# Token halves of K and V exchanged for half the units, so that 32-wide matmuls use eight array quadrants

## The chip, the cores and the metric

The kernel runs on one core of one Trainium2 chip. The metric is device time in microseconds (us), lower is better. Before the change three runs took 635.24, 636.76 and 638.88 us; their median is 636.76.

## The reference

Two stages follow each other. The first is a delta rule over 768 tokens for 4 batches and 8 heads of dimension 48, in fp32:

```python
k_n = k / (np.linalg.norm(k, axis=-1, keepdims=True) + 1e-06)
for t in range(S):
    y[:, :, t] = q[:, :, t] @ state
    v_old = state . k_n[:, :, t]
    state = state + beta * outer(k_n[:, :, t], v[:, :, t] - v_old)
```

The second is a gated MLP on the 3072 rows of y (width 384, inner width 1536): `out = (sigmoid(x @ w_gate) * (x @ w_val)) @ w_out`.

## The kernel before, in words

The 768 tokens are cut into N = 12 groups of 64. In a group there are 32 units (batch and head), named by e (0, 1), x (0, 1) and j (0 to 7); `tokens_at(e, x)` says on which half of the 128 partitions a unit's 64 tokens lie. Within a group the recurrence is written as matrix products, solved in two halves of 32 tokens:

- `gram` (line 282): K times K transposed into `pg` (line 291, 32 matmuls of 64x64). ACT copies its diagonal blocks to G (six copies, line 303) and its lower left blocks to L (four copies, line 308).
- `masked` (line 311): K times Q transposed into `pp` (line 319); DVE writes it back under a causal mask (line 324, four operations).
- `norms` and `solve` (DVE, lines 235 and 329): lengths of K, then the inverse of a triangular 32x32 matrix per unit and half, by some 62 small operations; the last one (line 352) transposes the result into `mt`.
- `rest` (line 434): K times the state into `pk` (line 446); `less` (line 454) subtracts it from V, which gives R.
- `updates` (line 459) in three steps. Step 0, the first U product: `mt` times R for the first 32 tokens into `pu` (line 477), copied to `su` by four ACT copies (line 483). Step 1, the L product: L times that U is added onto `pk` for the other 32 tokens (line 469), then `less` again. Step 2, the second U product.
- `rows` (line 485): Y. One kind of unit (x = 1) adds two products (line 503); the other (x = 0) has query and masked matrix stacked on 128 rows and is one matmul of 128 rows by 64 columns each (line 506, 16 matmuls).
- `advance` (line 514): the new state through `pd` (line 524).
- `turn` or `flip`: Y transposed into the MLP's input.

A matmul of 32 rows by 32 columns uses one of the array's sixteen 32x32 quadrants: its row block is given by where the operands lie, its column block by where the result goes. In steps 0 to 2 the 32 matmuls of a step go round four quadrants, since the four kinds (e, x) have four different row blocks and each always writes to one column block.

The MLP is what fills PE between these steps. A group has 24 slots: in an even slot `gate_val` (line 586) makes one tile of gate and value (`gv`, 18 matmuls), in an odd slot `outp` (line 617) adds one tile to the output (`po`, 6 matmuls). The sigmoid (ACT, line 591), the product (DVE, line 592), the split in two parts (ACT line 597, DVE line 602) follow it. The MLP of a group runs one group behind the recurrence. The order is written by hand: `plan[s]` holds what is issued in slot s right behind the matmuls, `late[s]` what comes last in it. From group 4 on, counted in slots of a period: `gram` of the next group and `rest` in slot 6, U in 9, L and the next group's `masked` in 11, the second U in 13, Y and the state in 15. Each engine works its own list off in order.

[...]

Of the kernel before, what the change touches and what calls it, by code (L numbers as in the profile page):

```python
# [12 lines left out]
F32 = mybir.dt.float32  # L13
# [8 lines left out]
PSUM = bass.MemoryType.PSUM  # L22

B, H, S, D = 4, 8, 768, 48
C = 64
GT = B * C
N = S // C
# [9 lines left out]
def tokens_at(e, x):  # L37
    return 64 * e if x else 64 - 64 * e


def head_of(e, x, j):

    return j // 2, (j % 2) * 4 + x * 2 + e
# [12 lines left out]
def deltanet_gated_mlp(ctx: ExitStack, tc: tile.TileContext, kd, qd, kv, beta, words, out):  # L56
# [4 lines left out]
    wt = ctx.enter_context(tc.tile_pool(name="wt", bufs=1))  # L61
    wk = ctx.enter_context(tc.tile_pool(name="wk", bufs=1))
    ps_seq = ctx.enter_context(tc.tile_pool(name="ps_seq", bufs=2, space=PSUM))
    ps_aux = ctx.enter_context(tc.tile_pool(name="ps_aux", bufs=2, space=PSUM))
    ps_gv = ctx.enter_context(tc.tile_pool(name="ps_gv", bufs=2, space=PSUM))
    ps_out = ctx.enter_context(tc.tile_pool(name="ps_out", bufs=2, space=PSUM))

# [214 lines left out]
    def gram(g):  # L282

        kq, st = kqp[g % 2], state[g]
        st["G"] = G = wk.tile([128, 32, CP], F32, name=f"G_{g}", tag="G", bufs=1)
        st["L"] = L = wk.tile([128, CP, 32], F32, name=f"L_{g}", tag="L", bufs=2)
        pg = [ps_aux.tile([128, J, C], F32, name=f"pg_{g}_{e}", tag="aux") for e in range(2)]
        for j in range(J):
            for e, x in KINDS:
                r, t = 64 * e, tokens_at(e, x)  # L290
                nc.tensor.matmul(out=pg[e][t:t + 64, j], lhsT=kq[r:r + D, x, j], rhs=kq[r:r + D, x, j], start=True, stop=True)  # L291
        return blocks_of(pg, G, L, g == 0)

    def blocks_of(pg, G, L, halves):
        for e in range(2):
            js = slice(e * J, (e + 1) * J)

            for lo, hi, o in ((0, 128, 0), (32, 64, 32), (96, 128, 32)):
                block = pg[e][lo:hi, :, o:o + 32].rearrange("q p t -> q t p")
                if halves and e:  # L300
                    nc.vector.tensor_copy(out=G[lo:hi, :, js], in_=block)
                else:
                    nc.scalar.copy(G[lo:hi, :, js], block)  # L303
                yield
        for e in range(2):
            for t in (0, 64):
                lo, o = t + 32 * e, 32 - 32 * e
                nc.scalar.copy(L[lo:lo + 32, e * J:(e + 1) * J], pg[e][lo:lo + 32, :, o:o + 32])
                yield

    def masked(g):

        kq = kqp[g % 2]
        pool, tag = (ps_aux, "aux") if g else (ps_out, "po")
        pp = [pool.tile([128, J, C], F32, name=f"pp_{g}_{e}", tag=tag) for e in range(2)]
        for j in range(J):
            for e, x in KINDS:
                r, t = 64 * e, tokens_at(e, x)
                nc.tensor.matmul(out=pp[e][t:t + 64, j], lhsT=kq[r:r + D, x, j], rhs=kq[r:r + D, 3 if x else 2 + 2 * e, j], start=True, stop=True)  # L319

        def masks():
            for e, x in sorted(KINDS):
                t, sec = tokens_at(e, x), 5 if x else 2 + 2 * e
                nc.vector.tensor_tensor(out=kq[t:t + 64, sec], in0=pp[e][t:t + 64],  # L324
                                        in1=pmask[t:t + 64, e].unsqueeze(1).to_broadcast([64, J, C]), op=ALU.mult)
                yield
        return masks()
# [45 lines left out]
    def solve_halves(g):  # L373
# [29 lines left out]
        pool, tag = (ps_aux, "aux") if g else (ps_gv, "gv")  # L403
        pz, pm = (pool.tile([128, CP, 32], F32, name=f"{n}_{g}", tag=tag) for n in ("pz", "pm"))

        def blocks(out, lhsT, rhs):
            for c in range(CP):
# [51 lines left out]
    def updates(g, step):  # L459

        st = state[g]
        R, L = st["R"], st["L"]

        at = {(e, x): [tokens_at(e, x) + 32 * (k ^ e) for k in range(2)] for e, x in KINDS}
        if step == 1:
            for j in range(J):
                for e, x in KINDS:
                    one, two = at[e, x]
                    nc.tensor.matmul(out=st["pk"][e][two:two + 32, j], lhsT=L[one:one + 32, e * J + j], rhs=su[one:one + 32, 3 if x else e, j],  # L469
                                     start=False, stop=True, skip_group_check=True)  # L470
            less(g)
            return
        pu = [ps_aux.tile([128, J, D], F32, name=f"pu_{g}_{step}_{x}", tag="aux") for x in range(1 if g else 2)]
        for j in range(J):
            for e, x in KINDS:
                r = at[e, x][step // 2]
                nc.tensor.matmul(out=pu[0 if g else x][r:r + 32, j], lhsT=mt[r:r + 32, e * J + j], rhs=R[e][r:r + 32, j], start=True, stop=True)  # L477
        for e, x in KINDS:
            r = at[e, x][step // 2]
            if g == 0 and x:  # L480
                nc.vector.tensor_copy(out=su[r:r + 32, 3 if x else e], in_=pu[1][r:r + 32])
            else:
                nc.scalar.copy(su[r:r + 32, 3 if x else e], pu[0][r:r + 32])  # L483

    def rows(g):

        st = state[g]
        kq = kqp[g % 2]

        py = [ps_aux.tile([128, 2, H // 2, D], F32, name=f"yy_{g}_{e}", tag="aux") for e in range(2)]  # L490

        def out_of(e, x, j):
            b, h = head_of(e, x, j)
            lo = 64 * (b % 2)
            return py[e][lo:lo + 64, b // 2, h // 2]
        order = [4 * hf + 2 * c + i for hf in range(2) for i in range(2) for c in range(2)]
        for pair in zip(order[::2], order[1::2]):
            for part in range(2) if g else (1,):
                for j in pair:
                    for e in range(2):  # L500
                        r = 64 * e
                        lhsT, rhs = ((kq[r:r + D, 3, j], su[r:r + D, 2, j]), (kq[r:r + 64, 5, j], su[r:r + 64, 3, j]))[part]
                        nc.tensor.matmul(out=out_of(e, 1, j), lhsT=lhsT, rhs=rhs, start=part == 0 or g == 0, stop=part == 1)  # L503
        for e in range(2):
            for j in order:
                nc.tensor.matmul(out=out_of(e, 0, j), lhsT=kq[:, 2 + 2 * e, j], rhs=su[:, e, j], start=True, stop=True)  # L506
# [26 lines left out]
    def flip(g, c):  # L533

        st = state[g]
        if c == 0:
            xx = wk.tile([128, 2, KC, GT], F32R if g else F32, name=f"xx_{g}", tag=f"xx{(g + 1) % 2}", bufs=1)
            st["xh"], st["xl"] = (xx[:, i] for i in range(2))
        xh, xl, ys = st["xh"], st["xl"], st["ys"][:, c].rearrange("p h e d -> p (h e d)")
        pt = ps_aux.tile([128, KC, 128], F32, name=f"pt_{g}_{c}", tag="aux")  # L540
# [209 lines left out]
    def mask_later(g, s):  # L750
        def fn():
            masks = masked(g)
            take(masks, 2)
            plan[s + 1].insert(0, steps(masks, 2))
        late[s].append(fn)
        for i in range(2):
            busy[s + i] += 1.4

    def gram_later(g, s):
        def fn():  # L760
            copies = gram(g)
# [120 lines left out]
```

## Time and profile before

| | |
|---|---|
| median of three runs | 636.76 us |
| the profiled execution's own time | 635.61 us |
| its span, first to last instruction | 633.9 us |
| PE, busy share of the span | 97% |
| mean granted PE clock | 0.998 |
| DMA, mean rate | 65 GB/s |

Times in the views are counted from the span's start. PE is TensorE's matmuls, PEld its weight loads, DVE VectorE, ACT ScalarE. A line of a group of instructions gives source line, engine, operation, output and inputs, shape, count, then busy time in us and the mean of one in ns, then the idle time ahead of them and what ended it. A row of the timeline begins with start and length in us; in the table of stretches the first numbers are the length and PE's busy time. An fp32 matmul appears as two records, so a step of 32 matmuls counts 64.

### The profile page before, as it was taken

The page shows a single profiled execution, that of the slowest core. Times are in us where ns is not written, and L with a number is a line of the kernel's source. Part 1 is how long each engine was busy: PE and PEld are TensorE (multiplying, and loading weights), DVE is VectorE, ACT ScalarE, POOL GpSimd, SP SyncE. Part 2 cuts the span into 40 slices and gives each one's busy share as a digit, 9 for nine tenths or more (in the row PEclk, how much of TensorE's full clock was granted, in tenths as well). Part 3 has the DMA queues.
Part 4 walks back from the last instruction along what each step waited for, and adds up shares of the span by engine and source line. Part 5 has one row for each costly group of instructions (what it writes and reads, how often), then busy time and mean ns, then how long its engine had stood idle before and what let it go on. Part 6 is the DMA issues. An engine that isn't in the chain of part 4 may idle for free.

```text
span 633.9 us, 24057 instructions
## 1 busy us (share of the span) xinstructions
PE 614.6 (97%) x10494; PEld 571.2 (90%) x10502; DVE 476.8 (75%) x1443; ACT 344.0 (54%) x933; POOL 39.6 (6%) x102
## 2 busy tenths in 40 slices
PE   6689999999999999999999999999999999999996
PEld 4367778989999999999999999999999999999996
DVE  5888897589977977977977977977987977953221
ACT  4879865567356356356355355355455455445222
POOL 6000000000002002002002002002002002001000
PEclk9999999999999999999999999999999999999999
DMA  9495831202203203103102102102112100100101
GB/s 271 177 296 181 277 91 54 53 2 87 52 3 86 52 4 86 42 12 86 45 11 86 34 21 87 27 28 86 26 29 86 26 4 3 26 3 2 26 1 25
DMA packets 17769, 41.06 MB, mean 65 GB/s; under 512 B 4224, under 2 KB 7296, under 8 KB 17664
## 3 DMA queue, kind: packets, MB, share of 16 engines
q1 hardware_dynamic: 17664, 39.53, 21.5%
q8 instruction: 82, 1.34, 0.9%
q14 instruction: 23, 0.19, 0.1%
HBM read 34.80 MB, written 4.72 MB: 62 GB/s over the span
## 4 chain that ended last, share of the span: by engine, by line
PE 91%; DVE 5%; ACT 1%; issue 1%; DMA 1%; ACTq 0%; SPq 0%; DVEq 0%
PE gv L586 45%; PE po L617 22%; PE gv L583 5%; PE pu L477 3%; PE po L611 3%; PE yy L503 2%; PE yy L506 2%; PE pk L446 2%; PE pg L291 2%; PE pp L319 2%; PE pd L524 2%; PE pk L469 1%; PE pm L409 1%; ACT su L483 1%; DVE kqp L324 1%
## 5 line engine op out<-in xcount | busy, mean ns | idle before, releaser
L586 PE MATMUL gv<-xx,w 128*128 128x256 f32 x2376 | 311.2, 285 | 0.0
L586 PEld LDWEIGHTS gv<-xx,w 128*128 128x128 f32 x2376 | 298.8, 191 | 3.1
L617 PE MATMUL po<-w,h 128*128 128x384 f32 x792 | 161.9, 340 | 0.0
L617 PEld LDWEIGHTS po<-w,h 128*128 128x128 f32 x792 | 133.8, 188 | 0.8
L597 ACT CAST h<-sg 128x256 fp32r<-128x256 f32 x132 | 53.5, 405 | 120.1 <-DVE sg L592 119.0
L591 ACT ACTIVATE sg<-gv 128x256 f32<-128x256 f32 x144 | 54.7, 380 | 107.8 <-PE gv L586 98.5
L592 DVE TENSOR_TENSOR sg<-sg,gv 128x256 f32<-128x256 f32 x144 | 60.1, 417 | 67.3 <-ACT sg L591 66.5
L350 DVE TENSOR_TENSOR X<-X,tmp 128x126 f32<-128x126 f32 (+22 forms) x279 | 71.1, 255 | 8.3
L347 DVE TENSOR_TENSOR tmp<-X,gp 128x126 f32<-128x126 f32 (+22 forms) x279 | 71.0, 254 | 8.3
L602 DVE TENSOR_TENSOR h<-sg,h 128x256 fp32r<-128x256 f32 x132 | 56.4, 428 | 13.2 <-ACT h L597 13.2
L562 POOL COPY x<-yt 32x192 f32<-32x192 f32 x72 | 28.3, 393 | 450.3 <-DVE yt L557 447.6
L279 ACT ACTIVATE kv<-kv,mq 128x48 f32<-128x48 f32 x192 | 47.9, 324 | 0.0
L483 ACT COPY su<-pu 32x384 f32<-32x384 f32 x92 | 43.3, 470 | 5.9 <-PE pu L477 4.1
L583 PE MATMUL gv<-xx,u 128*128 128x256 f32 x144 | 33.8, 385 | 0.7 <-issue 0.4
L324 DVE TENSOR_TENSOR kqp<-pp,pmask 64x512 f32<-64x512 f32 x48 | 32.3, 687 | 2.1 <-PE pp L319 1.1
L303 ACT COPY G<-pg 32x256 f32<-32x256 f32 (+1 forms) x69 | 25.3, 367 | 14.0 <-PE pg L291 12.7
L583 PEld LDWEIGHTS gv<-xx,u 128*128 128x128 f32 x144 | 26.6, 190 | 5.8 <-issue 0.8
L557 DVE STREAM_TRANSPOSE yt<-ys 128x768 f32<-128x768 f32 x9 | 8.8, 979 | 25.4 <-ACT ys L512 25.4
L457 DVE TENSOR_TENSOR R<-kv,pk 128x384 f32<-128x384 f32 x44 | 22.3, 549 | 6.6 <-PE pk L469 6.5
L562 ACT COPY x<-yt 32x192 f32<-32x192 f32 x72 | 25.2, 349 | 1.2
L212 ACT CAST w<-u 128x384 fp32r<-128x384 f32 x36 | 18.0, 508 | 8.1 <-DVE w L219 8.0
L531 DVE TENSOR_TENSOR su<-su,pd 48x384 f32<-48x384 f32 x40 | 21.7, 543 | 0.8 <-PE pd L524 0.4
(109 smaller groups left out, 556.2 us busy)
## 6 DMA issues: line engine op xcount, KB each, us to landing
raw<-in_words_dram SPq DMA_DIRECT2D x36, 384.0 KB, 5.5
kv<-in_kv_dram SPq DMA_DIRECT2D x24, 384.0 KB, 4.5
kqp<-in_qd_dram SPq DMA_DIRECT2D x24, 256.0 KB, 4.1
kqp<-in_kd_dram SPq DMA_DIRECT2D x24, 192.0 KB, 3.5
out_dram<-ot SPq DMA_DIRECT2D x48, 96.0 KB, 2.2
beta<-in_beta_dram SPq DMA_DIRECT2D x12, 16.0 KB, 4.0
```

Of the source, the lines that this page charges most:

```text
L279: nc.scalar.activation(V[:, c], V[:, c], AF.Copy, scale=mq[:, c, 0:1])
L347: nc.vector.tensor_tensor(out=tmp, in0=X[:, k:16, j:j + 1].to_broadcast([128, n, j]), in1=gp[:, j:j + 1, 0:j].to_broadcast([128, n, j]), o ...
L350: nc.vector.tensor_tensor(out=X[:, k:16, 0:j], in0=X[:, k:16, 0:j], in1=tmp, op=ALU.add)
L483: nc.scalar.copy(su[r:r + 32, 3 if x else e], pu[0][r:r + 32])
L562: copy(x[32 * q:32 * q + 32, :, :, a].rearrange("q k c s -> q c k s"), yt[32 * a:32 * a + 32, :, q::4])
L583: nc.tensor.matmul(out=pg[:, o], lhsT=parts[w, f][:, k * 128:(k + 1) * 128], rhs=x[0][:, k], start=k == 0, stop=k == KC - 1)
L586: nc.tensor.matmul(out=pg[:, o], lhsT=parts[w, f][:, a, k * 128:(k + 1) * 128], rhs=x[b][:, k], start=(k == 0 and q == 0), stop=(k == KC - ...
L591: nc.scalar.activation(h, st["gv", f][:, 0], AF.Sigmoid)
L592: nc.vector.tensor_tensor(out=h, in0=h, in1=st["gv", f][:, 1], op=ALU.mult)
L597: nc.scalar.copy(hh[:, 0], st["sg", f])
L602: nc.vector.tensor_tensor(out=hh[:, 1], in0=st["sg", f], in1=hh[:, 0].bitcast(F32), op=ALU.subtract)
L617: nc.tensor.matmul(out=po[s], lhsT=hh[:, a, ts], rhs=parts["o", f][:, w], start=(f == 0 and q == 0), stop=(f == NF - 1 and q == 2))
```

## The change

For groups 2 to 11, the units with j of 4 and more (`turned_over`) have the two 32-token halves of K (in `kd`), V and beta exchanged where the inputs are laid out; K by tokens, which `advance` reads, stays. Their U and L products then read another row block than their neighbours while they write the same column block, and the steps take the j in the order 0, 4, 1, 5, ..., so that eight quadrants follow each other. U's results of j below 4 and from 4 on go to two banks.

What goes with it: `ps_aux` becomes one buffer of two banks (`two_banks`), so pg, pp, pu, yy and pt each take both at once. L is copied in eight pieces of half the size. In `masked` a turned unit's product is made in two matmuls of 32 columns, which put its token halves back in order. In `rows` the stacked matmuls of every group but the first become two of 32 columns each. From group 4 on, `gram` stands one slot earlier (slot 5) and its copies are spread 6, 4, 4 over three slots; `masked` of group 3 moves by one slot.

```diff
+def turned_over(g, j):
+    return int(g > 1 and j >= J // 2)
...
-    ps_aux = ctx.enter_context(tc.tile_pool(name="ps_aux", bufs=2, space=PSUM))
+    ps_aux = ctx.enter_context(tc.tile_pool(name="ps_aux", bufs=1, space=PSUM))
...
+    def two_banks(name, *shape):
+        t = ps_aux.tile([128, 2, 512], F32, name=name, tag="aux")
+        n = int(np.prod(shape))
+        axes = "a b c"[:2 * len(shape) - 1]
+        return t, [t[:, i, 0:n].rearrange(f"q ({axes}) -> q {axes}", **dict(zip("abc", shape))) for i in range(2)]
...
             for t in (0, 64):
-                lo, o = t + 32 * e, 32 - 32 * e
-                nc.scalar.copy(L[lo:lo + 32, e * J:(e + 1) * J], pg[e][lo:lo + 32, :, o:o + 32])
-                yield
+                for j in (0, J // 2) if g > 1 else (0,):
+                    js = slice(j, j + J // 2) if g > 1 else slice(0, J)
+                    a = e ^ turned_over(g, j)
+                    nc.scalar.copy(L[t + 32 * e:t + 32 * e + 32, e * J + js.start:e * J + js.stop],
+                                   pg[e][t + 32 * a:t + 32 * a + 32, js, 32 - 32 * a:64 - 32 * a])
+                    yield
...
-                nc.tensor.matmul(out=pp[e][t:t + 64, j], lhsT=kq[r:r + D, x, j], rhs=kq[r:r + D, 3 if x else 2 + 2 * e, j], start=True, stop=True)
+                n = 32 if turned_over(g, j) else 64
+                for a in range(0, 64, n):
+                    b = 32 - a if n == 32 else 0
+                    nc.tensor.matmul(out=pp[e][t + a:t + a + n, j], lhsT=kq[r:r + D, x, j, b:b + n], rhs=kq[r:r + D, 3 if x else 2 + 2 * e, j],
+                                     start=True, stop=True)
...
+        order = [j for pair in zip(range(J // 2), range(J // 2, J)) for j in pair] if g else range(J)
         if step == 1:
-            for j in range(J):
+            for j in order:
                 for e, x in KINDS:
-                    one, two = at[e, x]
+                    one, two = at[e, x][0], at[e, x][1 - turned_over(g, j)]
...
-        pu = [ps_aux.tile([128, J, D], F32, name=f"pu_{g}_{step}_{x}", tag="aux") for x in range(1 if g else 2)]
-        for j in range(J):
+        both, pu = two_banks(f"pu_{g}_{step}", J // 2 if g else J, D)
+        for j in order:
             for e, x in KINDS:
-                r = at[e, x][step // 2]
-                nc.tensor.matmul(out=pu[0 if g else x][r:r + 32, j], lhsT=mt[r:r + 32, e * J + j], rhs=R[e][r:r + 32, j], start=True, stop=True)
+                r, i = at[e, x][step // 2], at[e, x][step // 2 ^ turned_over(g, j)]
+                nc.tensor.matmul(out=pu[j // 4 if g else x][r:r + 32, j % 4 if g else j], lhsT=mt[i:i + 32, e * J + j], rhs=R[e][i:i + 32, j], start=True, stop=True)
...
+        n = 32 if g else 64
         for e in range(2):
-            for j in order:
-                nc.tensor.matmul(out=out_of(e, 0, j), lhsT=kq[:, 2 + 2 * e, j], rhs=su[:, e, j], start=True, stop=True)
+            for pair in zip(order[::2], order[1::2]):
+                for a in range(0, 64, n):
+                    for j in pair:
+                        nc.tensor.matmul(out=out_of(e, 0, j, a, n), lhsT=kq[:, 2 + 2 * e, j, a:a + n], rhs=su[:, e, j], start=True, stop=True)
...
-            for i, n in enumerate((4, 2, 4) if g < 4 else (6, 4)):
+            for i, n in enumerate((4, 4, 6) if g < 4 else (6, 4, 4)):
                 plan[s + 1 + i].append(steps(copies, n))
...
-            gram_later(g, {2: 3, 3: 32}.get(g, w - 18))
-            mask_later(g, {2: 25, 3: 38}.get(g, w - 13))
+            gram_later(g, {2: 3, 3: 32}.get(g, w - 19))
+            mask_later(g, {2: 25, 3: 39}.get(g, w - 13))
```

In the changed kernel the same statements have other line numbers (302 for pg, 465 for rest, 338 for the mask product, 611 and 642 for the MLP; on ACT 314 and 321 for G and L, 616 for the sigmoid, 622 for the cast). PE's row around `rest` in a steady group, before (of each kind of matmul of a step the first two rows):

```order
L617 MATMUL po_0_5583<-w_1435,h_0_5498 128x384
L617 MATMUL po_1_5584<-w_1435,h_0_5498 128x384
L586 MATMUL gv_3_5599<-xx_5199,w_1682 128x256 x9
L586 MATMUL gv_3_5599<-xx_5199,w_1698 128x256 x9
L446 MATMUL pk_0_5623<-su,kqp_76 64x48
L446 MATMUL pk_1_5624<-su,kqp_76 64x48
L291 MATMUL pg_0_5663<-kqp_77 64x64
L291 MATMUL pg_1_5664<-kqp_77 64x64
L617 MATMUL po_0_5583<-w_1582,h_1_5550 128x384
```

And in the changed kernel:

```order
L642 MATMUL po_0_6646<-w_1431,h_0_6561 128x384
L642 MATMUL po_1_6647<-w_1431,h_0_6561 128x384
L302 MATMUL pg_6664<-kqp_76 64x64 x32
L611 MATMUL gv_3_6697<-xx_6262,w_1693 128x256 x9
L611 MATMUL gv_3_6697<-xx_6262,w_1709 128x256 x9
L465 MATMUL pk_0_6727<-su,kqp_77 64x48
L465 MATMUL pk_1_6728<-su,kqp_77 64x48
L642 MATMUL po_0_6646<-w_1578,h_1_6613 128x384
```

pg has moved from behind pk to between po and the fourth gate tile, so it no longer has a neighbour of its own shape. ACT's row at the same place, before:

```order
L597 CAST h_2_7345<-sg_2_7328 128x256
L591 ACTIVATE sg_3_7368<-gv_3_7347 128x256
L303 COPY G_7409<-pg_0_7411 128x32x8
L303 COPY G_7409<-pg_0_7411 32x32x8 x2
L303 COPY G_7409<-pg_1_7412 128x32x8
L303 COPY G_7409<-pg_1_7412 32x32x8 x2
L597 CAST h_3_7464<-sg_3_7368 128x256
L308 COPY L_7410<-pg_0_7411 32x256 x2
L308 COPY L_7410<-pg_1_7412 32x256 x2
L591 ACTIVATE sg_4_7490<-gv_4_7466 128x256
```

And in the changed kernel:

```order
L622 CAST h_2_7567<-sg_2_7550 128x256
L314 COPY G_7569<-pg_7571 128x32x8
L314 COPY G_7569<-pg_7571 32x32x8 x2
L616 ACTIVATE sg_3_7631<-gv_3_7604 128x256
L321 COPY L_7570<-pg_7571 32x128 x4
L622 CAST h_3_7689<-sg_3_7631 128x256
L616 ACTIVATE sg_4_7715<-gv_4_7691 128x256
```

The six copies of G stand ahead of the sigmoid of the fourth gate tile (sg_3) instead of behind it, and L's copies, now eight, lie on both sides of that tile's cast. (The rows for the second half of G and of L read like those shown.) The mask product's row on PE is, in the changed kernel, ahead of the gate tile of slot 12:

```order
L489 MATMUL pk_0_5820<-su,L_4849 32x48
L489 MATMUL pk_1_5821<-su,L_4849 32x48
L338 MATMUL pp_6029<-kqp_77 64x64 x16
L338 MATMUL pp_6029<-kqp_77 32x64 x32
L611 MATMUL gv_6_6080<-xx_5355,w_2148 128x256 x9
```

Before, it was 32 matmuls of 64x64 at that place; now 16 of them are left, and 32 of half the width stand behind them.

More of the change, by code (lines that the diff above doesn't have):

```diff
@@ L286, in gram @@
         st["L"] = L = wk.tile([128, CP, 32], F32, name=f"L_{g}", tag="L", bufs=2)
-        pg = [ps_aux.tile([128, J, C], F32, name=f"pg_{g}_{e}", tag="aux") for e in range(2)]
+        _, pg = two_banks(f"pg_{g}", J, C)
         for j in range(J):
@@ L291, in gram, with blocks_of @@
                 nc.tensor.matmul(out=pg[e][t:t + 64, j], lhsT=kq[r:r + D, x, j], rhs=kq[r:r + D, x, j], start=True, stop=True)
-        return blocks_of(pg, G, L, g == 0)
-    def blocks_of(pg, G, L, halves):
+        return blocks_of(g, pg, G, L)
+    def blocks_of(g, pg, G, L):
         for e in range(2):
@@ L299, in blocks_of @@
                 block = pg[e][lo:hi, :, o:o + 32].rearrange("q p t -> q t p")
-                if halves and e:
+                if g == 0 and e:
                     nc.vector.tensor_copy(out=G[lo:hi, :, js], in_=block)
@@ L306, in blocks_of @@
             for t in (0, 64):
-                lo, o = t + 32 * e, 32 - 32 * e
-                nc.scalar.copy(L[lo:lo + 32, e * J:(e + 1) * J], pg[e][lo:lo + 32, :, o:o + 32])
-                yield
+                for j in (0, J // 2) if g > 1 else (0,):
[4 more added lines that the diff above has]
+                    yield
     def masked(g):
         kq = kqp[g % 2]
-        pool, tag = (ps_aux, "aux") if g else (ps_out, "po")
-        pp = [pool.tile([128, J, C], F32, name=f"pp_{g}_{e}", tag=tag) for e in range(2)]
+        if g:
+            _, pp = two_banks(f"pp_{g}", J, C)
+        else:
+            pp = [ps_out.tile([128, J, C], F32, name=f"pp_{g}_{e}", tag="po") for e in range(2)]
         for j in range(J):
@@ L402, in solve_halves @@
         yield
-        pool, tag = (ps_aux, "aux") if g else (ps_gv, "gv")
-        pz, pm = (pool.tile([128, CP, 32], F32, name=f"{n}_{g}", tag=tag) for n in ("pz", "pm"))
+        pz, pm = (two_banks(f"{n}_{g}", CP, 32)[1][0] if g else ps_gv.tile([128, CP, 32], F32, name=f"{n}_{g}", tag="gv") for n in ("pz", "pm"))
         def blocks(out, lhsT, rhs):
@@ L472, in updates @@
             return
-        pu = [ps_aux.tile([128, J, D], F32, name=f"pu_{g}_{step}_{x}", tag="aux") for x in range(1 if g else 2)]
-        for j in range(J):
+        both, pu = two_banks(f"pu_{g}_{step}", J // 2 if g else J, D)
+        for j in order:
             for e, x in KINDS:
-                r = at[e, x][step // 2]
-                nc.tensor.matmul(out=pu[0 if g else x][r:r + 32, j], lhsT=mt[r:r + 32, e * J + j], rhs=R[e][r:r + 32, j], start=True, stop=True)
+                r, i = at[e, x][step // 2], at[e, x][step // 2 ^ turned_over(g, j)]
+                nc.tensor.matmul(out=pu[j // 4 if g else x][r:r + 32, j % 4 if g else j], lhsT=mt[i:i + 32, e * J + j], rhs=R[e][i:i + 32, j], start=True, stop=True)
         for e, x in KINDS:
             r = at[e, x][step // 2]
-            if g == 0 and x:
-                nc.vector.tensor_copy(out=su[r:r + 32, 3 if x else e], in_=pu[1][r:r + 32])
+            if g:
+                nc.scalar.copy(su[r:r + 32, 3 if x else e].rearrange("q (a j) d -> q a (j d)", a=2), both[r:r + 32, :, 0:J // 2 * D])
             else:
-                nc.scalar.copy(su[r:r + 32, 3 if x else e], pu[0][r:r + 32])
+                (nc.vector.tensor_copy if x else nc.scalar.copy)(out=su[r:r + 32, 3 if x else e], in_=pu[x][r:r + 32])
     def rows(g):
@@ L488, in rows, with out_of @@
         kq = kqp[g % 2]
-        py = [ps_aux.tile([128, 2, H // 2, D], F32, name=f"yy_{g}_{e}", tag="aux") for e in range(2)]
-        def out_of(e, x, j):
+        _, py = two_banks(f"yy_{g}", 2, H // 2, D)
+        def out_of(e, x, j, a=0, n=64):
             b, h = head_of(e, x, j)
-            lo = 64 * (b % 2)
-            return py[e][lo:lo + 64, b // 2, h // 2]
+            lo = 64 * (b % 2) + a
+            return py[e][lo:lo + n, b // 2, h // 2]
         order = [4 * hf + 2 * c + i for hf in range(2) for i in range(2) for c in range(2)]
@@ L539, in flip @@
         xh, xl, ys = st["xh"], st["xl"], st["ys"][:, c].rearrange("p h e d -> p (h e d)")
-        pt = ps_aux.tile([128, KC, 128], F32, name=f"pt_{g}_{c}", tag="aux")
+        if c == 0:
+            _, st["pt"] = two_banks(f"pt_{g}", KC, 128)
+        pt = st["pt"][c]
         for k in range(KC):
@@ L841, in units, with swapped @@
         return np.stack([x[head_of(e, kind, j)] for j in range(J)]).reshape(J, N, C, -1)
-    def swapped(x, e):
-        return x.reshape(J, N, 2, 32, -1)[:, :, ::-1].reshape(x.shape) if e else x
+    def swapped(x, e, turn):
+        halves = x.reshape(J, N, 2, 32, -1)
+        return np.stack([np.stack([halves[j, g, ::-1] if e ^ (turn and turned_over(g, j)) else halves[j, g] for g in range(N)]) for j in range(J)]).reshape(x.shape)
     def by_dim(x, swap):
@@ L851, in by_dim, with by_token @@
             kinds = [units(x, e, kind) for kind in ((0, 1) if swap or not e else (1, 0))]
-            rows.append(np.stack([swapped(u, e) if swap else u for u in kinds]))
+            rows.append(np.stack([swapped(u, e, True) if swap else u for u in kinds]))
         return np.ascontiguousarray(np.stack(rows).transpose(3, 0, 5, 1, 2, 4)).reshape(N, 2, -1, CP * C)
-    def by_token(x):
-        halves = [[swapped(units(x, e, int(half == e)), e) for e in range(2)] for half in range(2)]
+    def by_token(x, turn):
+        halves = [[swapped(units(x, e, int(half == e)), e, turn) for e in range(2)] for half in range(2)]
         return np.stack([np.stack(u) for u in halves]).transpose(3, 0, 4, 1, 2, 5)
@@ L863, in words_of @@
         return np.stack([g, v, w_out.reshape(NF, 128, PW)], axis=1).reshape(NF * 3, 128, PW).view(np.uint64)
-    kv_of = [by_token(x).reshape(N, 128, CP * D) for x in (k, v)]
-    bt = by_token(beta).reshape(N, 2, 2, 32, CP).transpose(1, 2, 4, 0, 3).reshape(NQ, 1, N, 32)
+    kv_of = [by_token(x, turn).reshape(N, 128, CP * D) for x, turn in ((k, False), (v, True))]
+    bt = by_token(beta, True).reshape(N, 2, 2, 32, CP).transpose(1, 2, 4, 0, 3).reshape(NQ, 1, N, 32)
     arrays = {
```

## The prediction

> **What bounds the kernel now.** First the page: how busy each engine is and what the chain that ended last is made of.
>
> ```profile
> span 633.9 us, 24057 instructions
> PE 614.6 (97%) x10494; PEld 571.2 (90%) x10502; DVE 476.8 (75%) x1443; ACT 344.0 (54%) x933; POOL 39.6 (6%) x102
> PE 91%; DVE 5%; ACT 1%; issue 1%; DMA 1%; ACTq 0%; SPq 0%; DVEq 0%
> ```
>
> PE is busy 97% of the span and makes up 91% of the chain. Next, two neighbouring stretches, each as long as one group of the steady part:
>
> ```profile
> 178.40:226.50 48.10, 48.10 (x834) 46.48 (x834) 39.37 (x122) 25.24 (x72) 3.18 (x8) 1.00 0.17 47
> 226.50:274.60 48.10, 48.10 (x834) 46.48 (x834) 39.47 (x122) 25.21 (x72) 3.18 (x8) 1.00 0.18 46
> ```
>
> PE (second number) is busy for all 48.10 us at full clock, DVE for 39.4, ACT for 25.2. So time taken from PE's own row comes off the end, and time added to it goes on, as long as DVE and ACT still hand over in time. Third, one group's row on PE, in order of time (start, length):
>
> ```profile
> 391.76 2.33 PE L586 MATMUL gv<-xx,w 128*128 128x256 f32 x18
> 394.98 2.33 PE L586 MATMUL gv<-xx,w 128*128 128x256 f32 x18
> 407.86 2.32 PE L586 MATMUL gv<-xx,w 128*128 128x256 f32 x18
> 410.11 1.15 PE L446 MATMUL pk<-su,kqp 48*64 48x48 f32 x64
> 411.08 1.13 PE L291 MATMUL pg<-kqp 48*64 48x64 f32 x64
> 412.13 1.32 PE L617 MATMUL po<-w,h 128*128 128x384 f32 x6
> 413.30 2.33 PE L586 MATMUL gv<-xx,w 128*128 128x256 f32 x18
> 416.61 0.88 PE L477 MATMUL pu<-R,mt 32*32 32x48 f32 x64
> 417.42 2.41 PE L586 MATMUL gv<-xx,w 128*128 128x256 f32 x18
> ```
>
> An undisturbed pair of slots (gv and po) lasts 394.98 - 391.76 = 3.22 us. With U between po and the next gv it lasts 417.42 - 413.30 = 4.12, so U costs 0.90. With pk and pg between gv and po it lasts 413.30 - 407.86 = 5.44, so the two cost 2.22.
>
> **The pace of small matmuls.** All terms need how fast records follow one another (an fp32 matmul here is two records). The groups:
>
> ```profile
> L477 PE MATMUL pu<-R,mt 32*32 32x48 f32 x1408 | 19.4, 203 | 0.0
> L409 PE MATMUL pz<-mt,scratch 32*32 32x32 f32 x256 | 2.6, 193 | 0.0
> L446 PE MATMUL pk<-su,kqp 48*64 48x48 f32 x704 | 12.6, 220 | 0.0
> L319 PE MATMUL pp<-kqp 48*64 48x64 f32 x768 | 15.6, 229 | 1.1 <-ACT su L483 0.8 <-DMA kqp<-in_qd_dram 0.3
> L506 PE MATMUL yy<-su,kqp 128*64 128x48 f32 x384 | 13.7, 224 | 0.0
> ```
>
> A step's length less its last record is the time over which its records start. U: 0.88 - 0.20 = 0.68 us for 64 records, 10.6 ns each; over four quadrants one quadrant takes 4 x 10.6 = 43 ns per record. pk: 1.15 - 0.22 = 0.93 for 64, 14.5 ns, 58 ns per quadrant. Y's stacked part: 384 records in 12 groups, 32 a group, 13.7/12 = 1.14 - 0.22 = 0.92, 28.7 ns, over two column halves again 58. So the array works on the tiles side by side and each has a pace of its own: 58 ns where the weights are 64 columns wide (with 48 and, below, with 64 moving columns), 43 where they are 32 wide. The fastest row is pz: 256 records in two groups, 2.6/2 = 1.3 - 0.19 = 1.11 us for 128, or 8.7 ns each.
>
> **U and L on eight quadrants.** Groups 2 to 11 turn half their units: 20 U steps and 10 L steps, each of 64 records over eight quadrants instead of four. L is U's equal:
>
> ```profile
> 420.81 0.88 PE L469 MATMUL pk<-su,L 32*32 32x48 f32 x64
> 421.63 1.16 PE L319 MATMUL pp<-kqp 48*64 48x64 f32 x64
> 422.72 2.41 PE L586 MATMUL gv<-xx,w 128*128 128x256 f32 x18
> 422.84 2.70 DVE L324 TENSOR_TENSOR kqp<-pp,pmask 64x512 f32<-64x512 f32 x4
> 426.11 0.88 PE L477 MATMUL pu<-R,mt 32*32 32x48 f32 x64
> ```
>
> If eight quadrants run at 43 ns each, a record comes every 5.3 ns and a step saves half of 0.68, 0.34 us. If they take turns it saves nothing. A loss has a reason against it: in pk every row half already feeds two column halves at the pace that Y's two halves have. No row shows records closer than pz's 8.7 ns, though its quadrants have less to stream; I take that as the pace at which matmuls are fed: 64 x (10.6 - 8.7) = 0.12 us a step, 30 x 0.12 = 3.7 us. The bounds are 0 and 10.2.
>
> [...]
>
> **Y by 32 columns.** Eleven groups: 32 stacked matmuls of 128x32 instead of 16 of 128x64, on four column tiles. With weights 32 wide the pace is U's: 64 records in 0.68 us instead of 32 in 0.92, so 0.24 less, 2.6 us in all. No row has four column tiles over all 128 rows; if only two were fed at a time it would be 64 x 43/2 = 1.38, 0.46 more, 5.1 us lost. U's four quadrants already use four column tiles, and row height made no difference between pk and Y, so I take the gain.
>
> **The mask product in two shapes.** In 10 groups half the units split their mask matmul by columns: 16 matmuls of 64 columns stay, 16 become 32 of 32 columns. The first half keeps 0.47 us; the second, 64 records at 8.7 ns, takes 0.56 instead of 0.47: +0.09. Between the halves the tile shape changes. What a change costs: pk, with its shape before and behind it pg's own, lasts 411.08 - 410.11 = 0.97 to the next start; pp, with a change on both sides, 422.72 - 421.63 = 1.09. So +0.11, together +0.20, 2.0 us in all. Bounds: nothing, if eight tiles run side by side and the narrower shape is no change; +0.58, if they run four at a time (0.94 for the half, +0.47) with the change.
>
> **The Gram product one slot earlier.** From group 4 on (8 groups) pg no longer stands next to pk but alone between po and gv, so the stream of large matmuls is broken once more. U's break cost 0.90 for 0.68 of records: 0.22. Eight times that is +1.8 us. The bounds are 0 and, from pk and pg together, 2.22 - 2 x 0.93 = 0.36 each.
>
> **Copies and waits.** These are hidden, each by a margin that can be read:
>
> ```profile
> 410.09 0.41 DVE L592 TENSOR_TENSOR sg<-sg,gv 128x256 f32<-128x256 f32 x1
> 410.53 0.40 ACT L597 CAST h<-sg 128x256 fp32r<-128x256 f32 x1 [2.75 <-DVE sg L592]
> 410.85 0.38 ACT L591 ACTIVATE sg<-gv 128x256 f32<-128x256 f32 x1
> 411.88 0.41 DVE L592 TENSOR_TENSOR sg<-sg,gv 128x256 f32<-128x256 f32 x1
> 412.25 2.31 ACT L303 COPY G<-pg 128x256 f32<-128x256 f32 x6 [1.03 <-PE pg L291]
> 414.02 0.71 DVE L352 STREAM_TRANSPOSE mt<-X 128x512 f32<-128x512 f32 x1
> 415.02 1.50 ACT L308 COPY L<-pg 32x256 f32<-32x256 f32 x4
> ```
>
> The six G copies now stand ahead of the sigmoid of the fourth gate tile, not behind it. ACT reaches them at about 410.85, when h's cast lets it (the earlier pg is done by then), and needs 2.31, so the sigmoid moves from 410.85 to 413.16 and DVE's product from 411.88 to about 413.55, 1.65 later. Queued behind that product on DVE are R, the last solve steps and mt, which U needs. mt ended at 414.73 and would end at 416.4; U starts at 416.61. Margin 0.2: no wait, but little cover. L's copies become eight of 128 instead of four of 256 elements; from 375 ns for 256 and 490 for su's 384 I estimate 0.26 us each, 2.1 instead of 1.5. Half of them now go before h's cast, so they end near 416.0; U, which now takes both PSUM banks and so waits for all of them, has 0.6 left. U's second step now waits for all four masks instead of the first two; they end at 425.54, before 426.11. The mask matmuls wait for U's copies in both banks, but L, ahead of them, needs the same copies.
>
> **Sum.** -3.7 (U, L) - 2.6 (Y) + 2.0 (mask) + 1.8 (Gram) = -2.5 us. The profiled execution took 635.61 (span 633.9 and 1.7 around it): 633.1. The median of the runs is 636.76, 1.15 above, which the range has to allow for. A measurement of this kernel can tell about 0.5%, 3.2 us, from no change.
>
> **The rivals.**
> Eight quadrants at their own pace: nothing feeds slower than 5.3 ns. -10.2 for U and L, -2.6, the mask +0.11 each or +1.1, Gram +1.8: -9.9, 625.7; halfway there, 629.4. For it: four quadrants keep the same pace as two halves. Against: pz at 8.7 ns. [...]
>
> Breaks that cost nothing: the mask's inner change and the lone pg are free. -3.7 - 2.6 + 0.9 = -5.4, 630.2. Against: pk's 0.97 beside pp's 1.09. [...]
>
> Slower, quadrants that take turns: two row groups that share a column group wait for one another's results, though in different banks. Then U and L gain nothing, and the mask's narrow half runs four at a time: -2.6 + 5.8 + 1.8 = +5.0, 640.6. It decides where eight quadrants' records come no closer than 10.6 ns. Against it: pk's two row halves share column halves at full pace.
>
> mt late: if ACT's copies hold DVE's product more than 1.9 us instead of 1.65, U waits. At 0.6 us in 8 groups it is +4.9 on the sum, 638.0. For it: 0.2 us of margin.
>
> A floor per matmul: 32-column matmuls are fed no faster than U's are now, 0.68/32 = 21 ns, so U and L gain nothing while the rest of the sum stands: -2.6 + 2.0 + 1.8 = +1.2, 636.8. Against: pz's 17 ns.
>
> **How the numbers follow.** The sum as it stands: 0.50 (of it 0.12 beyond 0.5% faster, 0.36 within, 0.02 slower). Eight at full or half pace: 0.15, faster. Free breaks: 0.15, faster. Quadrants in turns: 0.09, slower. mt late: 0.07, within 0.5%. The floor: 0.04, within. Faster 0.12 + 0.15 + 0.15 = 0.42; same 0.36 + 0.07 + 0.04 = 0.47; slower 0.02 + 0.09 = 0.11. The likeliest case alone spans 630.5 to 636. The range goes from 628.8, which leaves out the better half of the eight-quadrant case (0.08), to 638.0, which takes in mt late and leaves out the quadrants in turns (0.09).
>
> **What would show it.** Right: U and L at about 0.76 instead of 0.88 us; yy's narrow part near 0.90 for 64 records; pp near 1.35 in two shapes; pg alone, with gv to gv about 0.2 longer over the two breaks; PE still without idle before pu. Wrong: U at 0.55 (full pace) or 0.88 (turns); pp above 1.6; idle on PE before pu with DVE mt or ACT L as releaser.

## The result and the profile after

The changed kernel takes 666.25 us (median of four runs, 662.91 to 667.99) beside 636.61 (635.24 to 638.88) of the kernel before: ratio 1.0456, 95% interval 1.0402 to 1.0509. It is 4.6% slower, where 633.1 us was forecast and 638.0 was the upper end. The span of the profiled execution went from 633.9 to 661.2 us, so 27.3 us have to be found.

The page after, first what answers to the page before: span, busy shares and the chain, then one line that the prediction did not look at, the queue that brings PE its instructions (packets, MB).

```profile
span 661.2 us, 25428 instructions
PE 622.5 (94%) x11166; PEld 572.2 (87%) x11174; DVE 476.5 (72%) x1443; ACT 349.6 (53%) x973; POOL 39.7 (6%) x102
PE 88%; DVE 6%; issue 3%; ACT 2%; DMA 1%; ACTq 0%; SPq 0%; DVEq 0%
q8 instruction: 87, 1.43, 0.9%
```

The same line on the page before:

```profile
q8 instruction: 82, 1.34, 0.9%
```

PE works 622.5 us instead of 614.6, 7.9 more, so most of the 27.3 us is idle time on PE. "Issue" in the chain, time in which an engine waits for nothing that the profile shows, rose from 1% to 3%. The queue's packets have 1.34 MB / 82 = 16 KB; PE has 10494 + 10502 instructions before and 11166 + 11174 after, and 1.34 and 1.43 MB over these counts are 64 bytes for each, before as after. So the packets are PE's own instructions, in pieces of 256, that is of 128 matmul records with their weight loads.

What PE waited for in the changed kernel (total us, times, longest):

```profile
PE pp L338 <- issue: 5.2, 4, 1.8
...
PE gv L611 <- issue: 3.5, 5, 1.5
PE pd L547 <- issue: 3.3, 5, 1.3
PE pt L567 <- DVE xx L573: 3.1, 2, 2.0
...
PE pu L497 <- DVE kqp L344: 2.4, 1, 2.4
PE yy L523 <- DVE su L503: 1.1, 1, 1.1
...
PE pt L567 <- ACT xx L570: 0.9, 1, 0.9
```

In the kernel before, of these only yy's wait for su is among PE's waits, with 0.3. They are of two kinds: waits without a releaser in the steady part, and waits for copies and masks in the first groups.

One group's row on PE in the changed kernel (start, length):

```profile
424.65 2.32 PE L611 MATMUL gv<-xx,w 128*128 128x256 f32 x18
426.82 1.22 PE L642 MATMUL po<-w,h 128*128 128x384 f32 x6
427.97 1.16 PE L302 MATMUL pg<-kqp 48*64 48x64 f32 x64
429.06 2.42 PE L611 MATMUL gv<-xx,w 128*128 128x256 f32 x18
431.41 1.15 PE L465 MATMUL pk<-su,kqp 48*64 48x48 f32 x64
432.49 1.32 PE L642 MATMUL po<-w,h 128*128 128x384 f32 x6
433.65 2.33 PE L611 MATMUL gv<-xx,w 128*128 128x256 f32 x18
...
436.96 0.80 PE L497 MATMUL pu<-R,mt 32*32 32x48 f32 x64
437.69 2.42 PE L611 MATMUL gv<-xx,w 128*128 128x256 f32 x18
...
441.10 0.80 PE L489 MATMUL pk<-su,L 32*32 32x48 f32 x64
441.83 1.45 PE L338 MATMUL pp<-kqp 48*64 48x64 f32 x93
445.05 0.30 PE L338 MATMUL pp<-kqp 48*32 48x64 f32 x3 [1.76 <-issue]
445.28 2.42 PE L611 MATMUL gv<-xx,w 128*128 128x256 f32 x18
...
453.90 0.89 PE L529 MATMUL yy<-su,kqp 128*32 128x48 f32 x64
454.71 1.11 PE L547 MATMUL pd<-su,kv 64*48 64x48 f32 x64
```

The steps themselves did about what was forecast (U: 0.73 to the next start instead of 0.81; Y's narrow part 0.81). The new thing is the hole in the mask product: 93 records, 1.76 us of nothing, then the last three. Counted over PE's instructions, every such hole of the steady part lies at the same remainder of 256 (185 or 186 in the changed kernel's trace, counted over matmuls, weight loads, 64 semaphore instructions and 3 drains). Summed by starts (each gap less the usual gap between the same two kinds of record), the holes at those places make 13.6 us after 150 us, where the kernel before has none. The queue shows the other side: in the thirteen traces of this case there are 126 places from 25 us on where PE stops without a releaser and, by starts, loses over 0.15 us, and at every one of them PE goes on 1.2 to 1.6 us after an instruction packet has ended; no two packets start under 3.3 us apart.

### The profile page after: what moved, and what is told of

Its sections match the earlier page's. It is cut to its first block, busy times and chain, and to the rows that moved or that the text cites. A ratio compares the mean times of both kernels' runs of the same rounds, so it can differ in the third digit from the quotient of the medians.

```text
span 661.2 us, 25428 instructions
## 1 busy us (share of the span) xinstructions
PE 622.5 (94%) x11166; PEld 572.2 (87%) x11174; DVE 476.5 (72%) x1443; ACT 349.6 (53%) x973; POOL 39.7 (6%) x102
## 3 DMA queue, kind: packets, MB, share of 16 engines
q8 instruction: 87, 1.43, 0.9%
## 4 chain that ended last, share of the span: by engine, by line
PE 88%; DVE 6%; issue 3%; ACT 2%; DMA 1%; ACTq 0%; SPq 0%; DVEq 0%
PE gv L611 43%; PE po L642 20%; PE gv L608 5%; PE pu L497 3%; PE po L636 2%; PE pp L338 2%; PE pk L465 2%; PE pg L302 2%; PE yy L523 2%; PE pd L547 2%; PE yy L529 1%; PE pk L489 1%; DVE w L230 1%; PE pz L110 1%; PE pm L428 1%
## 5 line engine op out<-in xcount | busy, mean ns | idle before, releaser
L611 PE MATMUL gv<-xx,w 128*128 128x256 f32 x2376 | 314.5, 286 | 3.5 <-issue 3.5
L501 ACT COPY su<-pu 32x384 f32<-32x384 f32 x88 | 41.4, 471 | 8.8 <-PE pu L497 7.5
L344 DVE TENSOR_TENSOR kqp<-pp,pmask 64x512 f32<-64x512 f32 x48 | 32.3, 686 | 11.0 <-PE pp L338 10.6
L338 PE MATMUL pp<-kqp 48*32 48x64 f32 (+1 forms) x1088 | 19.5, 229 | 5.6 <-issue 5.2
L321 ACT COPY L<-pg 32x128 f32<-32x128 f32 (+1 forms) x88 | 23.4, 265 | 2.4 <-DVE G L312 1.4
```

Source lines behind the costliest of these rows:

```text
L501: nc.scalar.copy(su[r:r + 32, 3 if x else e].rearrange("q (a j) d -> q a (j d)", a=2), both[r:r + 32, :, 0:J // 2 * D])
L611: nc.tensor.matmul(out=pg[:, o], lhsT=parts[w, f][:, a, k * 128:(k + 1) * 128], rhs=x[b][:, k], start=(k == 0 and q == 0), stop=(k == KC - ...
```

## The experiments

Theory "supply": PE's instructions come in pieces of 128 records, the next piece takes some 3.5 us to be there, and where PE uses up a piece faster it stops. L and the mask product now follow each other with 64 + 96 = 160 records in about 2.2 us, Y's two parts and the state update with 192 in 2.8. Rival "shape": narrow tiles, or two row blocks on one column block, are slow by themselves. Theory "tile", for the first groups: with one tile over two banks, whoever needs one bank waits for the user of the other.

**y_narrow**: the kernel before with only Y's stacked part by 32 columns.

```diff
-            for j in order:
-                nc.tensor.matmul(out=out_of(e, 0, j), lhsT=kq[:, 2 + 2 * e, j], ...)
+            for pair in zip(order[::2], order[1::2]):
+                for a in range(0, 64, n):
+                    for j in pair:
+                        nc.tensor.matmul(out=out_of(e, 0, j, a, n), lhsT=kq[:, 2 + 2 * e, j, a:a + n], ...)
```

> The kernel before, with one part of the change alone: the stacked Y matmuls of groups 1 to 11 in 32 columns. Theory 'supply': PE's instructions arrive in pieces of 256 (128 records), and where a whole piece is used up by small matmuls in under some 3.6 us PE stands still until the next is there. Then the narrow Y itself takes 0.82 instead of 1.07 us in 11 groups (-2.7), but its run with pd grows from 160 to 192 records, so some stops come back: 633 to 640 us, and every stop lies a multiple of 128 records from the others. Rival 'shape' (narrow tiles and tiles that share columns are slow by themselves): no stops, and the time follows the step's own length, 634.

Measured: 640.23 us, ratio 1.0084 [1.0060, 1.0109], span +3.6. Its waits of PE:

```profile
PE pd L527 <- issue: 3.6, 3, 1.3
...
PE gv L589 <- issue: 1.5, 2, 0.7
```

In groups without a hole the next group comes 0.2 to 0.3 us earlier against the kernel before, as Y's 1.07 to 0.82 us asks for. The four holes after 150 us (at 151, 290, 483 and 533 us), 5.1 us together, take back more than the 2.7 us that Y gains. A step that became faster made the kernel slower.

**mask_twice**: the kernel before, the second half of the mask product made twice, in its old shape.

```diff
+        for j in range(J // 2 if g > 1 else J, J):
+            for e, x in KINDS:
+                r, t = 64 * e, tokens_at(e, x)
+                nc.tensor.matmul(out=pp[e][t:t + 64, j], lhsT=kq[r:r + D, x, j], rhs=kq[r:r + D, 3 if x else 2 + 2 * e, j], start=True, stop=True)
```

> The kernel before, with 16 of the 32 mask matmuls of groups 2 to 11 made a second time, same shape, same place, same result: L and the mask product together are 160 records instead of 128, as in the change, with nothing narrow in it. Supply: +4.7 us for the records themselves, and on top stops of 0.5 to 2 us behind or in the mask product, 5 to 12 us in all: 646 to 653. Shape: +4.7 us and no stop, 641.

Measured: 645.91 us, 1.0180 [1.0137, 1.0222], span +9.1. The added records are 10 x 32 at 14.5 ns, 4.6 us. Most of the other 4.5 are holes: 5.4 us at borders of pieces, where the kernel before has 1.3 (by starts, from 60 us on). Two rows of its waits:

```profile
PE gv L590 <- issue: 1.6, 2, 1.0
PE pp L323 <- issue: 1.3, 1, 1.3
```

There is no narrow tile and no turned unit in it. That speaks against "shape" as the maker of the holes.

**two_tiles**: the changed kernel with two tiles of one bank each; U's results are copied per bank.

```diff
-        t = ps_aux.tile([128, 2, 512], F32, name=name, tag="aux")
...
+        return None, [ps_aux.tile([128, *shape], F32, name=f"{name}_{i}", tag="aux") for i in range(2)]
...
-                nc.scalar.copy(su[r:r + 32, 3 if x else e].rearrange(...), both[r:r + 32, :, 0:J // 2 * D])
+                for a in range(2):
+                    nc.scalar.copy(su[r:r + 32, 3 if x else e, a * 4:a * 4 + 4], pu[a][r:r + 32])
```

> The changed kernel, with the pair of PSUM banks as two tiles of one bank in two buffers, as before, instead of one tile of two banks; U's results are copied by eight copies of half the size. Theory 'tile' (what uses one bank of a two-bank tile waits for what uses the other: in the first groups the transposes, U behind the masks, ACT and DVE copies of one step): 5 to 9 us of the 30 come back, nearly all of it before 185 us, 657 to 661. If the tile makes no difference: 666.

Measured: 651.75 us, 1.0261 [1.0224, 1.0298], span +14.5 on before and 12.8 less than the changed kernel, more than the 5 to 9 expected. The waits on pt for these copies are gone and yy's is 0.3 again; the wait for the mask stays (2.0 in 2). The U that starts at 176 us in the kernel before comes 3.9 us later, in the changed kernel 10.6. Not all of the 12.8 is the tile's: its holes at borders after 150 us make 6.2 us instead of 13.6, since the same order of work with other tiles and other waits meets the borders elsewhere.

**not_turned**: the changed kernel with no unit turned (four quadrants again, the mask product in one shape); tile, Y and Gram as changed.

```diff
-    return int(g > 1 and j >= J // 2)
+    return 0
```

> The changed kernel with no unit turned over: U and L on four quadrants, the mask product whole (32 matmuls). Supply: the 160 records of L and mask are 128 again, so the stops there go (about 8 us), those behind Y and pd stay; the mask gets 3.2 shorter, U and L 2.4 longer: 655 to 660. Shape: -0.8 us for the steps, 665, apart from the mask's own excess.

Measured: 654.04 us, 1.0295 [1.0270, 1.0319]. U and L are back at 0.81 us, the mask product at 1.09, so those sizes belong to the turning. The stops in the mask product went, all but 0.3 us, and the time came out a little below the 655 to 660 expected. The total does not price the turning: other holes moved to the state update ("PE pd <- issue" 5.0 us in 4).

**long_run**: the kernel before, the mask product of group 6 made nine times in a row, to see PE's supply by itself.

```diff
-        for j in range(J):
+        for j in list(range(J)) * (9 if g == 6 else 1):
```

> The kernel before, with one mask product (group 6) made nine times over at its place, same shape and result: one run of 64 + 576 = 640 small records on PE, 512 of them extra. Supply: once what is on hand is used up, PE gets 128 records per piece and a piece every 3.9 us, with stops of about 2 us in between at every 128th record; the extra 512 records last about 4 x 3.9 = 16 us instead of 512 x 14.5 ns = 7.4. If PE alone set the pace: 7.4 us and no stops.

Measured: 649.21 us (one run). Its row on PE:

```profile
276.49 0.88 PE L469 MATMUL pk<-su,L 32*32 32x48 f32 x64
277.30 1.67 PE L319 MATMUL pp<-kqp 48*64 48x64 f32 x97
280.05 2.09 PE L319 MATMUL pp<-kqp 48*64 48x64 f32 x128 [1.08 <-issue]
283.50 2.09 PE L319 MATMUL pp<-kqp 48*64 48x64 f32 x128 [1.36 <-issue]
286.96 2.09 PE L319 MATMUL pp<-kqp 48*64 48x64 f32 x128 [1.36 <-issue]
290.41 1.62 PE L319 MATMUL pp<-kqp 48*64 48x64 f32 x95 [1.36 <-issue]
```

This settles the mechanism. All matmuls are alike and wait for nobody, yet PE stops after every 128 records, and restarts every 286.96 - 283.50 = 3.46 us (3.9 was expected). In this stretch one piece arrives per 3.46 us; 128 records at 14.5 ns are used in 1.9. The instruction queue's packets in the trace start 3.5 to 3.7 us apart there and take 0.9 to 1.2 us each, so most of the 3.46 is not the transfer. The first stop comes 161 records after the step L began, so there is about one piece in hand, no more.

It also explains the holes of the changed kernel. In its row above, the first record behind the hole starts 3.76 us after the one 128 records ahead of it, which lies in L; the two other holes inside the mask product give 3.42 and 3.36. Over all 13 holes after 150 us it is 2.3 to 3.8 us: less than 3.46 where the piece was already there when PE reached it.

**shifted**: two_tiles with 32 tiny matmuls more at about 16 us, while PE is idle. They are bf16 matmuls, one record and one weight load each (as in the kernel before at line 441, where two calls leave 2 records and 2 loads), so they shift every border of a piece by 32 records (64 instructions) against the steps; the steps of the groups stay as they are, and what they write is overwritten.

```diff
+            for _ in range(32):
+                nc.tensor.matmul(out=pz.rearrange("q a b -> q (a b)")[:, 0:16], lhsT=flat[:, 0:128], rhs=flat[:, 0:16], start=True, stop=True)
```

> The variant with two tiles, with 32 tiny matmuls (64 instructions) put in at about 16 us, where PE stands idle anyway. Supply: every later piece border moves by 32 records against the steps, so the stops that it had in the mask product at 235, 287 and 338 us move to other steps, shrink or grow, while their remainder by 128 records stays the same; 643 to 656 us. If the stops were those of the step itself (a wait, a shape): the same stops at the same steps, 652.

Measured: 644.81 us, 1.0148 [1.0111, 1.0184], span 642.7 instead of two_tiles' 648.4. More work, less time. The same steps as in the row above, in this run:

```profile
425.62 0.80 PE L496 MATMUL pu<-R,mt 32*32 32x48 f32 x64
426.35 2.42 PE L611 MATMUL gv<-xx,w 128*128 128x256 f32 x18
...
429.76 0.80 PE L488 MATMUL pk<-su,L 32*32 32x48 f32 x64
430.49 1.50 PE L335 MATMUL pp<-kqp 48*64 48x64 f32 x96
431.93 2.42 PE L611 MATMUL gv<-xx,w 128*128 128x256 f32 x18
...
440.55 0.89 PE L529 MATMUL yy<-su,kqp 128*32 128x48 f32 x64
441.37 0.94 PE L547 MATMUL pd<-su,kv 64*48 64x48 f32 x64
```

The mask product, two shapes and 160 records with L, runs through in 1.44 us. From 160 us to the end there is no hole at all, and U's start drifts only 0.2 us a group against the kernel before. So the steps as such are nearly neutral, and "shape" falls as the cause of the loss. The price is paid earlier: a border that now falls into the `pm` of group 1's solve costs 2.8 us at 68 us.

**mask_apart**: two_tiles with the mask product one slot earlier, no longer behind L.

```diff
-            mask_later(g, {2: 25, 3: 39}.get(g, w - 13))
+            mask_later(g, {2: 25, 3: 39}.get(g, w - 14))
```

> The variant with two tiles, with the mask product of groups 4 to 11 one slot earlier, so that a gate and an output tile stand around it and the run of 160 records behind L is cut into 96 and 64. Supply: the stops in the mask product (about 5 us) go, one more break of the stream costs 0.3 us in 8 groups: 647 to 650. Shape: no gain, plus the breaks, 654.

Measured: 648.45 us, 1.0209 [1.0177, 1.0241], span 645.4, 3.0 less than two_tiles. The holes in the mask product are gone; small ones (0.2 to 0.8 us) at L, Y and the state update are left, and the stream of large matmuls is broken once more in each group.

**gram_back**: two_tiles with the Gram product in its old slot and L's copies in the two slots behind it.

```diff
-            for i, n in enumerate((4, 4, 6) if g < 4 else (6, 4, 4)):
+            for i, n in enumerate((4, 4, 6) if g < 4 else (6, 8)):
...
-            gram_later(g, {2: 3, 3: 32}.get(g, w - 19))
+            gram_later(g, {2: 3, 3: 32}.get(g, w - 18))
```

> The variant with two tiles, with the Gram product back in its old slot behind rest, copies 6 and 8. Measured on the timelines, pg alone costs 0.33 us more a group than beside pk: 8 groups, -2.7 us if U need not wait for the L copies; pk and pg are then a run of 128 records, which may bring a stop or two back. 648 to 651; if the copies hold U up, 652 or more.

Measured: 655.64 us, 1.0320 [1.0298, 1.0343], span 4.7 more than two_tiles. Part of it is a wait that the moved Gram product avoids, in each of eight groups:

```profile
PE pu L494 <- ACT L L318: 2.6, 8, 0.3
```

By starts it is 0.52 us in each, 4.2 in all. Holes in the mask product come on top (5.5 us in 5 instead of 3.1 in 3), and what the Gram product gains by standing beside pk comes off. So the Gram product's earlier slot was not a free choice: U now takes both banks, and L's eight copies must have left them.

**one_tile**: the kernel before in order, shapes and copies, with one auxiliary tile over two banks.

```diff
-    ps_aux = ctx.enter_context(tc.tile_pool(name="ps_aux", bufs=2, space=PSUM))
+    ps_aux = ctx.enter_context(tc.tile_pool(name="ps_aux", bufs=1, space=PSUM))
...
-        pg = [ps_aux.tile([128, J, C], F32, name=f"pg_{g}_{e}", tag="aux") for e in range(2)]
+        pg = two_banks(f"pg_{g}", J, C)
```

> The kernel before in everything but its auxiliary PSUM tiles: one tile over two banks, as the changed kernel has it, in place of two of one bank; the order of the work, the shapes and the copies stay those of before. Tile theory: users of one bank now wait for users of the other. In the first groups the flips, U and Y wait for DVE's and ACT's copies, 6 to 13 us by group 4; from group 4 on the Gram product is still one slot later than in the changed kernel, so U waits for the L copies, about 0.5 us in 8 groups; in all 9 to 17 us over the kernel before (645 to 652), with waits of PE on pt, pu and yy in the profile. Supply theory alone (all of the loss is PE without instructions): the tile changes nothing in PE's instructions, within 2 us of the kernel before.

Measured: 644.68 us, 1.0128 [1.0093, 1.0164], span +6.2. Its waits have the same rows as the changed kernel's:

```profile
PE pt L548 <- DVE xx L554: 3.2, 2, 2.0
PE yy L507 <- DVE su L485: 1.1, 1, 1.1
...
PE pt L548 <- ACT xx L551: 0.9, 1, 0.9
```

At the same U (176 us before) the delay is 6.3 us, and it stays at 6.3 to the end; the span is 6.2 longer. So the tile costs 6.2 us, all in the first groups, most of it where Y is turned by PE (`flip`): the second flip's bank belongs to the same tile as the first's, which DVE is still reading. The lower end was expected there; the wait of U for L's copies in later groups, also expected, did not come, since the four larger copies end in time.

**after_shifted**: the changed kernel with the same 32 tiny matmuls.

> The changed kernel with 32 tiny matmuls more near its start, which move the borders of the 128-record pieces by 64 records and change no step. The same 32 took 5.7 us of span from the variant with two tiles. If the loss to the tile and the loss to supply are apart, the changed kernel gets 6 to 13 us faster (653 to 660) and the steady part shows no stops of PE without a releaser, while the waits on pt, su and yy before 150 us stay. If the stops are made by what the tile does, the time stays at 664 to 668.

Measured: 654.00 us, 1.0263 [1.0224, 1.0301], span 652.1, 9.1 less than the changed kernel. No hole over 0.15 us is left behind 170 us; from that U to the last one the delay grows from 17.1 to 18.5 us, where the changed kernel's grows from 10.6 to 27.6. Up to that U it pays 6.5 us more than the changed kernel, in part in holes at `pm` (2.8 us) and the state update (1.0). The waits on pt (3.1 and 0.9), yy (1.1) and on the mask (2.4) stay. So the two losses are apart, as the first case expected (the shift is 32 records, as in shifted, and not the 64 that the expectation names).

**y_shifted**: y_narrow with the same 32 tiny matmuls, the one attempt at a kernel faster than both.

> The kernel before with Y's stacked part by 32 columns (the run y_narrow) and the same 32 tiny matmuls near its start. Supply theory: its period is 6.5 and a half pieces still (848 records, not a whole number of 128), so borders fall on every step in turn; moving them by 64 records takes the stops at the state update away in some groups and brings them in others: 635 to 641. If all its stops go: about 634, faster than the kernel before by 1 to 2 us. Shape theory (narrow tiles slow by themselves): 640 as y_narrow.

Measured: 644.37 us, 1.0118 [1.0089, 1.0146], outside both expectations. The holes did not go, they moved: `pm` 2.8 us at 67 us, and four at the state update, 4.7. The shift and the period in that text are wrong too. The tiny matmuls are 32 records, not 64; Y's 16 added matmuls are 32 records, so the period is 832 + 32 = 864, 6.75 pieces, and the borders go through four places in turn; no shift takes all of them out of the dense stretches. The changed kernel's 832 + 32 + 32 = 896 is 7 pieces, which is why one shift could clear all its groups, and why without it the holes come back in every group. No version of the change that ran beats the kernel before.

## Why the prediction was wrong, by its own steps

**What bounds the kernel: the step that failed.** The prediction held that time taken from PE's row comes off the end "as long as DVE and ACT still hand over in time". That left out a third supplier, PE's own instructions. 128 records must last about as long as a piece takes to come, 3.46 us in long_run; a group's gate and output matmuls, 24 records in 3.22 us, are far from that, but the small-matmul steps use a piece in under 2. In the kernel before, a dense stretch is L and the mask product, 128 records, and its period of 832 records, 6.5 pieces, let no border cost anything after 150 us. The kernel before was not run with its borders moved, so how far that is luck of where they lie is not shown. The change made the dense stretches both longer (160 and 192 records) and faster, and its period of 7 pieces put the borders into them group after group. That cost 13.6 us of holes. Behind the hole at 543.9 us the granted clock also fell (length, PE, ..., PEclk):

```profile
525.00:550.00 25.00, 23.63 (x473) 22.17 (x472) 18.25 (x58) 10.90 (x31) 0.00 (x0) 0.93 0.08 19
```

0.07 x 25 = 1.75 us more. In two_tiles the same happened at its holes of 1.7 and 1.5 us:

```profile
225.00:250.00 25.00, 23.47 (x590) 21.79 (x587) 15.35 (x42) 11.38 (x38) 0.00 (x0) 0.93 0.09 21
275.00:300.00 25.00, 23.68 (x589) 21.86 (x587) 15.51 (x46) 12.58 (x42) 0.00 (x0) 0.93 0.07 19
```

Not every hole of that size is followed by it (those at 392.9 and 443.3 us in the changed kernel are not). Why some are stays open.

**"Copies and waits ... hidden": wrong in the first groups, right behind them.** The prediction priced the tile over two banks in the steady part alone. There the mt wait did not come, and U's second step did not wait for its four masks. In the first groups, with other steps and another spacing, the tile cost 6.2 us (one_tile), and the second U of group 2 waited 2.4 us for the mask of group 3, whose product the change puts one slot later while U now needs both banks.

**The terms of the sum.** From first start to the next step's first start, median of groups 3 to 10, in the kernel before and in shifted, which has no holes there:

| term | before | now | times | measured | forecast |
|---|---|---|---|---|---|
| U and L | 0.81 | 0.73 | 30 | -2.4 | -3.7 |
| Y by 32 columns | 1.07 | 0.82 | 11 | -2.8 | -2.6 |
| mask in two shapes | 1.09 | 1.43 | 10 | +3.4 | +2.0 |
| Gram alone | 8.66 | 8.99 | 8 | +2.6 | +1.8 |

The Gram row is the stretch over two slots: 5.44 + 3.22 before, 433.65 - 424.65 = 9.00 in the row above. Sum +0.8 instead of -2.5: without the tile and without a single hole the steps would still have gained nothing. U and L gained, but less than forecast: over a step eight quadrants run neither at their own 5.3 ns nor in turns at 10.6. In the trace U's first 32 records follow 6 to 7 ns apart; then come a gap of 0.1 us and matmuls every 17 ns, 8.5 a record, near the 8.7 taken from pz, whose matmuls also start 17 ns apart over four quadrants. That this pace is the one at which matmuls are fed was the author's estimate; no run shows it. The gap is what the forecast did not have. Y is right. In the mask product the change of shape within the step cost the 0.11 us of the forecast: the 32nd and the 33rd record start 0.149 us apart in after_shifted, where no hole lies in the step, and 0.038 apart in the kernel before. Mis-sized was the narrow half: its 64 records start over 0.64 us, where 0.56 was forecast, and the 32 that they replace over 0.43 and not 0.47. The lone Gram product cost 0.33 us a group instead of 0.22, within its bound of 0.36. Of the rivals, "free breaks", "own pace" and "turns" are refuted by this table, and the floor per matmul too, since 32 matmuls now take 0.73 us.

**The account of the 27.3 us.** Steps +0.8, tile +6.2, second U of group 2 +2.4, holes after 150 us +13.6, reduced clock +1.75, holes at borders from 60 to 150 us 2.8 instead of 1.3, +1.5: 26.3. The rest, about 1 us, lies in part in the first groups: over 30 to 40 us the granted clock of this execution is 0.83, where the kernel before and one_tile have 1.00, and the U at 34.5 us of the kernel before comes 2.9 us later, in one_tile 1.6. The tile's 6.2 is shown by a run that adds it alone, the holes by runs that take them out of the steady part; the 2.4, the clock and the early holes are read from the trace only, and some of the parts before 150 us may overlap.

## What to carry to other kernels

Before making a run of small matmuls faster or longer, count PE's instructions: any 256 of them that PE can use up in less than about the 3.46 us measured here may end in a stop, and whether they do hangs on where in the count they lie, so that a harmless edit elsewhere moves the time by a per cent (32 tiny matmuls: 651.75 to 644.81 us). Spread small matmuls between large ones rather than packing steps together (mask_apart: 3.0 us less of span), and read "issue" waits at equal remainders of the instruction count as supply, not as shape. Two banks in one tile are one resource (6.2 us in one_tile): price the edit in the start-up groups too, where the spacing is not that of the steady part.

## What the hardware showed that was not expected

- PE gets its instructions in packets of 16 KB, one per 3.46 us in long_run, with about one in hand. A packet itself mostly takes 0.9 to 1.6 us, and a PE that stopped for it goes on 1.2 to 1.6 us after it has ended.
- 32 tiny matmuls added at the start made the changed kernel 9.1 us shorter and its two-tile variant 5.7, but left y_narrow longer by 4.2 in span.
- Matmuls of 32x32 on eight quadrants start 13 ns apart for the first 16, then, behind a gap of 0.1 us, 17 ns apart (U at 436.96 us in the changed kernel); on four they also start 17 ns apart in pz.
- Passing from 64 to 32 columns within the mask product costs 0.11 us (0.149 instead of 0.038 us between two starts). The larger part of its +0.34 is the narrow half itself, 64 records in 0.64 us instead of 32 in 0.43.
